# A copy on ScalarE moved behind the scores and exponentials of head 13

## The chip, the cores and the metric

The kernel runs on one core of a Trainium2 chip. A core has engines that each run their own list of instructions in order and meet through semaphores: TensorE (PE in the profile; its weight loads are PEld), VectorE (DVE), ScalarE (ACT), GpSimd (POOL) and SyncE (SP), which here only issues DMAs. Sixteen DMA engines move data between device memory and the core's buffers. The metric is the device time of one execution in microseconds (us); lower is better.

## The reference

Attention with a gate for each of 8 batches and 8 heads (576 positions, head size 64), and then a layer norm and an MLP with a residual on the 512 joined columns:

```python
scores = scale * np.matmul(q, k.transpose(0, 1, 3, 2))
cum = np.cumsum(np.maximum(s, 0.0), axis=-1)
bias = -(cum[:, :, :, None] - cum[:, :, None, :])
scores = np.where(causal, -1e9, scores + np.minimum(bias, 0.0))
attn = softmax(scores)                       # by row
x = join_heads(np.matmul(attn, v))           # (8, 576, 512)
xn = (x - mean) / np.sqrt(var + 1e-6) * g_ln
out = x + np.maximum(xn @ w_ch1, 0.0) @ w_ch2
```

The condensed lines `softmax` and `join_heads` stand for the reference's own lines; inputs and output are float32.

## The kernel before

All of the work is written out by hand as one list of short words, `PLAN` (lines 1274 to 1356). A loop at the end of `fast_path` (1357) takes word after word and calls the function that `STEPS` (1191) has for it. Nothing reorders the instructions later: the order of the words is the order in which each engine gets its instructions, and two steps on different engines are tied only where one reads or overwrites what the other uses. Where an engine's next instruction waits, all of its later ones wait.

Batch 0 is worked in tiles of 128 positions, batch 1 in single heads 8 to 15, batches 2 to 7 in pairs of heads (a burst of scores for two heads at once). Matmuls of the MLP for batches that are done stand between the attention steps, as units in a queue; a word `u` or `U` takes the next one. Eight batches of MLP units follow one another to the end of the kernel.

The words that matter here:

- `d.12`, `d.14`: `scores_d` (420), scores and exponentials of the last 64 positions of two heads: a matmul for each head into the tile `sd`, and one exponential on ACT (line 437).
- `s.12` to `s.15`: `scores` (382), one head's scores: five matmuls (line 390) into three PSUM banks `sa`, `sb`, `sc`, and on ACT one exponential for each (line 401), from the bank into the buffer `er`. There are three banks in all for these tiles, so the scores of one head wait for the exponentials of the head before. For heads 10 and up POOL then puts zeros over the masked part (lines 410 and 440).
- `v.12` and so on: `pv` (573), the product of those exponentials with the values, in `pot` (line 583); `n.12`: its norm on DVE (595 to 604).
- `u`, `U`: one MLP unit. In the first half four matmuls into `ph` (`mlp1`, line 761) and a ReLU on ACT (`u`, line 752) or DVE (`U`, line 750); in the second half four matmuls into `py` (`mlp2`, line 780) and after every fourth unit the output on DVE (`yo`, line 792) and a store.
- `lp.9`: `ld_cast_pair` (185) issues on POOL the loads of the keys and queries of head pair 9 into `kp` and `qp`. Pairs 8 to 11 are the pairs of batch 2. `w2.3` (`ld_w2`, line 255) issues on POOL the load of the last quarter of the second MLP weight.
- `O2.k.9`: `side_two` (342), on the engine named after the colon. It copies a loaded pair so that the two heads lie side by side, into a part of `rowb`; the copy itself is the one line 140, 142 or 144 of `copy_on`. In the profile it is `rowb<-kp` or `rowb<-qp`.
- `F.k.9`: `tr_two` (355), six transposes on PE of that part of `rowb` into `trp` (line 360). `G.k.9`: `evac_two` (365), a copy of `trp` to the place that batch 2's bursts read (`kq<-trp`).
- `lv`, `lr`: loads of value, key and query rows of later batches through SP's queue (line 205). `vm`: `weigh_v` (229) on POOL, value rows times weights into `v_bf` (line 232). `cr`: casts of key or query rows on POOL (line 217).
- `tk.2`: `tail_keys` (502), POOL's copies into `kz` of the last 64 keys of batch 2 (line 144). `sd.2`: `tails` (514), PE's scores from them (line 519); `se.2` and `sm.2`: exponential (532) and mask on POOL. `bm`: POOL's masks of a burst (line 492).
- `B2.8`: `burst` (541), scores of pair 8 (line 548); `bx`: its exponentials (553); `Y.8.0`, `Y.8.1`: the products with the values of its two heads, numbers 16 and 17 (line 627).

In this part of the list `O2.k.9` is the first of eight such copies, one for each of the keys and queries of pairs 8 to 11. It comes right after the copies of head pair 7's transposed queries and ahead of the scores of head 12:

```python
def side_two(kind, g, eng):
    o = (2 * g + "kq".index(kind)) % 4 * 2 * QT * D
    x = rowb.rearrange("p t h c -> p (t h c)")[:, o : o + 2 * QT * D].rearrange(
        "p (t h d) -> p t h d", t=QT, h=2
    )
    copy_on(eng, x[0:QP], ready.pop((kind, g))[0:QP].rearrange("p h (t d) -> p t h d", t=QT))
    sided[kind, g] = x
```

Of the kernel before, what the change touches and what calls it, by code (L numbers as in the profile page):

```python
# [30 lines left out]
def fast_path(  # L31
# [13 lines left out]
    B, H, S, D = q.shape  # L45
# [891 lines left out]
    E = {"A": "act", "D": "dve", "P": "pool"}  # L937
# [241 lines left out]
    def raise_flag(count, ones, n):  # L1179
# [106 lines left out]
        Q.q.5 r.0.2:D B.1.0 s.8 u X.3 S.4.1.0 x.4.1.0 y.3:D Sk xk E.q.5.1:D E.q.5.0:A B.0.0 B.3.0 a3 u  # L1286
        v.8 qu.4 qu.5 Q.k.5 lp.9 E.k.5.0:D u E.k.5.1:D V.4.0 N.4.0 s.9 cr.3.0.1 n.8 V.4.1 N.4.1 Q.q.6
        E.q.6.0:A u B.2.0 d.10 s.10 wr Q.k.6 E.k.6.0:D A.0 v.9 lp.10 w2.2 lr.3.1 E.k.6.1:D n.9 u U
        E.q.6.1:A s.11 Q.k.7 Q.q.7 E.q.7.0:A lp.11 La.6 E.k.7.0:D E.q.7.1:A U U O2.k.9:A E.k.7.1:D v.10
        n.10 cr.3.0.0 U d.12 s.12 U v.11 n.11 ga.1.0.0 A.2 d.14 s.13 u w2.3 B.3.1 v.12 n.12 ga.1.0.3  # L1290
        s.14 O2.k.8:A A.1 me wT lv.2.0 wx vo.2:P U v.13 n.13 ga.1.1.2 s.15 cr.3.1.1 U O2.q.9:A ga.1.0.2
        F.k.8 v.14 vm.2.0:P ga.1.0.1 F.k.9 G.k.9:A n.14 U u A.3 lr.3.2 v.15 cr.3.2.0 O2.k.11:A lv.2.1
        lv.2.2 R vm.2.1:P G.k.8:A ga.1.1.1 u lv.2.3 u O2.q.8:A ga.1.1.3 F.q.9 G.q.9:A n.15 ga.1.2.1
# [260 lines left out]
def kernel(tc, q, k, v, s, g, w1, w2, out):  # L1554
    nc = tc.nc
    with tc.tile_pool(name="flag", bufs=1) as pool:
        flag = pool.tile([1, 1], I32, name="flag")
        bad = fast_path(tc, q, k, v, s, g, w1, w2, out, flag)
        with tc.If(bad > 0, preferred_fallthrough_block=False):
            general_path(tc, q, k, v, s, g, w1, w2, out)  # L1560
# [28 lines left out]
```

## Time and profile before

| what | value |
|---|---|
| median of 3 runs | 351.22 us (349.23, 351.22, 352.59) |
| the profiled execution | 351.01 us, of which the span of the instructions is 349.5 us |
| mean granted TensorE clock in it | 0.987 of full speed |
| read from device memory, written to it | 37.11 MB, 9.44 MB |
| `rowb<-kp` copies on ACT | 4, of 829 to 832 ns |
| exponentials `er<-sa`, `er<-sb`, `er<-sc` | about 0.6 us each, the next starting 0.48 us after |

Busy time of an engine counts its own instructions, not its waits. Times inside the profile are microseconds from the start of the span. The chain of waits is followed back from the last instruction of all: at each step to what released it. A row of a timeline has the start, the duration, the engine, the line, the operation, what it writes and reads with sizes, and in brackets the idle time of the engine before it and what ended that. Matmuls are pipelined, so that the durations of neighbouring rows overlap. The granted clock is the share of full speed that the clock of TensorE had in a stretch; the DMA share is the mean busy share of the 16 DMA engines, which passes 1 where transfers overlap on an engine.

### The profile page before, as it was taken

To read this page: it belongs to the slowest core of one execution; us is meant where nothing else is said; L and a number is where in the kernel's file an instruction comes from. 1 tells how busy PE (TensorE), PEld (TensorE's weight loads), DVE (VectorE), ACT (ScalarE), POOL (GpSimd) and SP (SyncE) were. 2 spreads that over 40 slices of the span, in tenths; PEclk is the share of its full clock that TensorE was granted. 3 is DMA by queue.
4 is the path that set the end of the run, shared out by engine and by line. 5 is a ranking of instruction groups with operands and counts; after the bars stand their busy time and mean duration, and the time that the engine had idled before them with its cause. 6 is when DMAs were issued, how large, how long until landed. Compare 5 with 4: busy or idle time off the path is not lost.

```text
span 349.5 us, 8012 instructions
## 1 busy us (share of the span) xinstructions
PE 334.0 (96%) x3066; PEld 185.7 (53%) x3092; DVE 207.4 (59%) x592; ACT 185.7 (53%) x343; POOL 167.9 (48%) x306
## 2 busy tenths in 40 slices
PE   6999988989999999999999999999999999999994
PEld 2998744545554555545554554555545444444443
DVE  6688894956666577456753765567257714433512
ACT  4688858767773778347665675386534303302200
POOL 8898755877477775865687176440301001000000
PEclk9899998999999999999999999999999999999998
DMA  9999999989997899999766958500230040011022
GB/s 150 182 190 172 202 194 212 188 222 218 221 203 155 210 212 208 194 232 224 164 150 172 216 112 187 123 18 2 89 93 0 3 150 32 14 60 61 0 64 66
DMA packets 147485, 48.61 MB, mean 139 GB/s; under 512 B 135184, under 2 KB 142896, under 8 KB 147440
## 3 DMA queue, kind: packets, MB, share of 16 engines
q1 hardware_dynamic: 121616, 38.34, 50.5%
q0 software_dynamic: 24304, 8.92, 21.5%
q10 hardware_dynamic: 1520, 0.79, 0.9%
q8 instruction: 25, 0.41, 0.5%
q14 instruction: 20, 0.16, 0.2%
HBM read 37.11 MB, written 9.44 MB: 133 GB/s over the span
## 4 chain that ended last, share of the span: by engine, by line
PE 88%; DMA 5%; DVE 2%; issue 1%; ACT 1%; POOL 1%; SPq 0%; ACTq 0%
PE py L780 36%; PE ph L761 32%; PE pot L627 7%; DMA kp<-in_k_dram 4%; PE sa L548 2%; PE ph L1068 2%; PE sc L548 2%; PE sb L548 2%; PE trt L944 1%; DMA c_in<-in_s_dram 1%; PE st L966 1%; PE trp L360 1%; PE pot L583 1%; PE pot L1024 0%; PE st L974 0%
## 5 line engine op out<-in xcount | busy, mean ns | idle before, releaser
L780 PE MATMUL py<-w_bf,hT 128*128 128x512 bf16 (+2 forms) x583 | 128.3, 367 | 2.3 <-DVE yo L792 0.8
L761 PE MATMUL ph<-xT,w_bf 128*128 128x512 bf16 x480 | 110.7, 381 | 0.0
L752 ACT ACTIVATE hT<-ph 128x512 bf16<-128x512 f32 x97 | 58.1, 603 | 81.6 <-PE ph L761 80.2
L780 PEld LDWEIGHTS <-hT 128*128 128x128 bf16 x608 | 56.0, 98 | 61.7 <-issue 1.3
L761 PEld LDWEIGHTS <-w_bf 128*128 128x128 bf16 x544 | 51.2, 98 | 56.8 <-issue 0.6
L492 POOL TENSOR_SCALAR_AFFINE_SELECT er<-er 128x256 bf16<-128x256 bf16 x96 | 38.6, 416 | 60.8 <-ACT er L553 45.8
L792 DVE SCALAR_TENSOR_TENSOR yo<-py,rstd,xb 128x512 f32<-128x512 f32 x32 | 23.9, 750 | 49.8 <-PE py L780 42.1
L750 DVE TENSOR_SCALAR hT<-ph 128x512 bf16<-128x512 f32 x39 | 26.7, 690 | 26.6 <-PE ph L761 25.9
L553 ACT ACTIVATE er<-sb 128x512 bf16<-128x512 f32 x48 | 28.2, 609 | 21.1 <-PE sb L548 20.2
L553 ACT ACTIVATE er<-sa 128x512 bf16<-128x512 f32 x48 | 28.6, 609 | 13.7 <-PE sa L548 10.9
L232 POOL TENSOR_TENSOR v_bf<-rowtmp,wt 128x512 bf16<-128x512 f32 (+1 forms) x30 | 32.0, 1072 | 1.1 <-DMA rowtmp<-in_v_dram 0.9
L553 ACT ACTIVATE er<-sc 128x512 bf16<-128x512 f32 x48 | 28.7, 613 | 4.1 <-PE sc L548 4.1
L627 PEld LDWEIGHTS <-er 128*128 128x128 bf16 x672 | 25.7, 97 | 9.5 <-issue 0.6
L627 PE MATMUL pot<-v_bf,er 128*128 128x66 bf16 x672 | 28.0, 193 | 0.1
L684 POOL TENSOR_TENSOR rstd<-rstd,mhalf 128x4 f32<-128x4 f32 (+1 forms) x8 | 8.8, 1098 | 38.2 <-DVE rstd L683 34.4
L644 DVE TENSOR_REDUCE sums<-pot 128x5 f32<-128x10 f32 x48 | 7.9, 165 | 30.5 <-PE pot L627 30.2
L710 DVE SCALAR_TENSOR_TENSOR xn<-xb,mv,gb 128x512 bf16<-128x512 f32 x28 | 24.0, 858 | 1.0
L669 DVE BATCH_NORM_STATS2 stats<-xb 128x6 f32<-128x128 f32 (+1 forms) x84 | 23.8, 323 | 0.4
L217 POOL CAST kq<-rowtmp 128x512 bf16<-128x512 f32 (+1 forms) x30 | 19.3, 652 | 9.6 <-DMA rowtmp<-in_k_dram 9.4
L647 DVE TENSOR_TENSOR xb<-pot,rinvs 128x256 f32<-128x256 f32 x48 | 20.4, 424 | 1.6
L548 PEld LDWEIGHTS <-kq 64*128 64x128 bf16 x360 | 11.2, 94 | 10.1 <-issue 4.7
L983 ACT ACTIVATE er<-st 128x512 bf16<-128x512 f32 x24 | 13.1, 604 | 3.5 <-PE st L974 2.4
(169 smaller groups left out, 398.3 us busy)
## 6 DMA issues: line engine op xcount, KB each, us to landing
out_dram<-yo SPq DMA_DIRECT2D x32, 256.0 KB
rowtmp<-in_v_dram SPq DMA_DIRECT2D x24, 256.0 KB
rowtmp<-in_k_dram SPq DMA_DIRECT2D x20, 256.0 KB
rowtmp<-in_q_dram SPq DMA_DIRECT2D x20, 256.0 KB
w_bf<-in_moe_w_ch_dram POOLq DMA_DIRECT2D x8, 512.0 KB, 8.6
kp<-in_k_dram POOLq DMA_DIRECT2D x8, 144.0 KB, 10.3
qp<-in_q_dram POOLq DMA_DIRECT2D x8, 144.0 KB, 10.6
v_bf<-in_v_dram POOLq DMA_DIRECT2D x8, 128.0 KB, 7.4
```

What stands on the lines that cost most here:

```text
L232: e.tensor_tensor(out=v_bf[b % 2][0:pn, t, :, 0:D], in0=loaded.pop(("v", b, t))[0:pn], in1=wt[0:pn, t, b, :].unsqueeze(2).to_broadcast([pn ...
L492: nc.gpsimd.affine_select(out=out, in_=out, compare_op=ALU.is_ge, fill=0.0, base=0, pattern=pattern, channel_multiplier=-1,)
L548: nc.tensor.matmul(a, lhsT=lhsT, rhs=rhs, start=True, stop=True)
L553: nc.scalar.activation(out=er[:, 2 * n % 4 + i, o : o + 512], in_=bank["B", n].pop((name, i)), func=ACT.Exp, scale=scale,)
L627: nc.tensor.matmul(pot[:, t, :], lhsT=cols, rhs=v_bf[b % 2][:, kb, h, :], start=(kb == 0), stop=(kb == t),)
L669: nc.vector.bn_stats(out=st[b][:, t, part, :], in_=x_tiles(b)[t][:, lo:hi])
L710: nc.vector.scalar_tensor_tensor(out=xn, in0=tiles[t], scalar=mvs[b][:, t, 0:1] if b > 0 else mean0[:, t : t + 1], in1=gb, op0=ALU.subtrac ...
L750: nc.vector.tensor_scalar_max(out=dst, in0=ph, scalar1=0.0)
L752: nc.scalar.activation(out=dst, in_=ph, func=ACT.Relu)
L761: nc.tensor.matmul(ph, lhsT=w1_bf[:, kd, fb * P : (fb + 1) * P], rhs=xT[:, :, kd, :], start=(kd == 0), stop=(kd == KD - 1),)
L780: nc.tensor.matmul(py[t], lhsT=hT[:, fb, t * P : (t + 1) * P], rhs=w2_bf[:, fb, c0:c1], start=(fb == 0), stop=(fb == FB - 1),)
L792: nc.vector.scalar_tensor_tensor(out=yo, in0=py[t], scalar=rs, in1=x[:, c0:c1], op0=ALU.mult, op1=ALU.add)
```

## The change

One word moves in the list: `O2.k.9:A`, the copy of the keys of head pair 9 (the second pair of batch 2). It goes from its place ahead of `E.k.7.1:D` (DVE's copy of pair 7's keys) to one behind `s.13`. On ACT it passes the exponentials of `d.12`, `s.12`, `d.14` and `s.13`, eight instructions. The words between keep their order, and no function changes. The reader of the copy, `F.k.9`, stays where it is, behind `s.15`.

```diff
-        E.q.6.1:A s.11 Q.k.7 Q.q.7 E.q.7.0:A lp.11 La.6 E.k.7.0:D E.q.7.1:A U U O2.k.9:A E.k.7.1:D v.10
-        n.10 cr.3.0.0 U d.12 s.12 U v.11 n.11 ga.1.0.0 A.2 d.14 s.13 u w2.3 B.3.1 v.12 n.12 ga.1.0.3
+        E.q.6.1:A s.11 Q.k.7 Q.q.7 E.q.7.0:A lp.11 La.6 E.k.7.0:D E.q.7.1:A U U E.k.7.1:D v.10 n.10
+        cr.3.0.0 U d.12 s.12 U v.11 n.11 ga.1.0.0 A.2 d.14 s.13 O2.k.9:A u w2.3 B.3.1 v.12 n.12 ga.1.0.3
         s.14 O2.k.8:A A.1 me wT lv.2.0 wx vo.2:P U v.13 n.13 ga.1.1.2 s.15 cr.3.1.1 U O2.q.9:A ga.1.0.2
         F.k.8 v.14 vm.2.0:P ga.1.0.1 F.k.9 G.k.9:A n.14 U u A.3 lr.3.2 v.15 cr.3.2.0 O2.k.11:A lv.2.1
```

## The prediction

> **What bounds the kernel now.** I began with the shares of busy time and the chain of waits on the page. TensorE (PE) is busy nearly everywhere and carries the chain, but one piece of the chain is no engine's work: the landing of a key pair.
>
> ```profile
> PE 334.0 (96%) x3066; PEld 185.7 (53%) x3092; DVE 207.4 (59%) x592; ACT 185.7 (53%) x343; POOL 167.9 (48%) x306
> ...
> PE 88%; DMA 5%; DVE 2%; issue 1%; ACT 1%; POOL 1%; SPq 0%; ACTq 0%
> PE py L780 36%; PE ph L761 32%; PE pot L627 7%; DMA kp<-in_k_dram 4%; PE sa L548 2%; PE ph L1068 2%; PE sc L548 2%; PE sb L548 2%; PE trt L944 1%; DMA c_in<-in_s_dram 1%; PE st L966 1%; PE trp L360 1%; PE pot L583 1%; PE pot L1024 0%; PE st L974 0%
> ```
>
> So a microsecond taken from a gap of PE shortens the kernel, if no later gap takes its place. Next, ScalarE's (ACT's) timeline around that landing (start, duration, line, what, idle time before and who ended it):
>
> ```profile
> 46.18 1.63 ACT L140 COPY kq<-trqk 64x576 bf16<-64x576 bf16 x2
> 52.03 0.83 ACT L140 COPY rowb<-kp 96x768 bf16<-96x768 bf16 x1 [4.23 <-DMA kp<-in_k_dram]
> 52.89 0.27 ACT L437 ACTIVATE er<-sd 64x128 bf16<-64x128 f32 x1
> 53.06 0.58 ACT L401 ACTIVATE er<-sa 128x512 bf16<-128x512 f32 x1
> ```
>
> The second row is the copy that the change moves. ACT stands 4.23 us before it, and the exponentials of head 12 stand behind it. PE's timeline shows who pays:
>
> ```profile
> 49.49 1.03 PE L761 MATMUL ph<-xT,w_bf 128*128 128x512 bf16 x4
> 50.36 0.62 PE L583 MATMUL pot<-v_bf,er 128*128 128x65 bf16 x15
> 50.81 0.22 PE L426 MATMUL sd<-kq 68*128 68x64 bf16 x2
> 53.69 0.59 PE L390 MATMUL sa<-kq 68*128 68x512 bf16 x1 [2.66 <-ACT er L401]
> ...
> 55.04 1.91 PE L761 MATMUL ph<-xT,w_bf 128*128 128x512 bf16 x4
> 56.75 0.75 PE L583 MATMUL pot<-v_bf,er 128*128 128x65 bf16 x15
> ```
>
> Head 13's scores need a score bank (there are three) that head 12's first exponential frees at 53.64. And what follows is slow: four matmuls of L761 take 1.91 us, before the gap 1.03. The table by stretches (PE busy, granted clock, DMA share, GB/s) gives the reason:
>
> ```profile
> 50.80:53.70 2.90, 0.24 (x9) 0.99 1.24 194
> 53.70:55.20 1.50, 1.50 (x6) 0.50 1.23 196
> 55.20:56.20 1.00, 1.00 (x4) 0.50 1.24 191
> 56.20:57.00 0.80, 0.80 (x7) 0.50 1.26 209
> 57.00:57.50 0.50, 0.50 (x16) 0.97 1.25 235
> ```
>
> The clock is at half from 53.7 to 57.0. The DMA share stays over 1.2 with and without PE: loads flow at their own pace here. The last view is GpSimd's (POOL's) timeline, 12 us on, where one of them is waited for:
>
> ```profile
> 66.11 1.04 POOL L232 TENSOR_TENSOR v_bf<-rowtmp,wt 128x512 bf16<-128x512 f32 x1
> 67.10 1.17 POOL L217 CAST kq<-rowtmp 128x512 bf16<-128x512 f32 x2
> 69.22 2.04 POOL L232 TENSOR_TENSOR v_bf<-rowtmp,wt 128x512 bf16<-128x512 f32 x2 [0.95 <-DMA rowtmp<-in_v_dram]
> 71.28 1.00 POOL L217 CAST kq<-rowtmp 128x512 bf16<-128x512 f32 x1
> 73.07 1.40 POOL L144 COPY kz<-kq 64x256 bf16<-64x256 bf16 x2 [0.80 <-ACT kq L140]
> ```
>
> **The change part by part.** *The wait that goes.* The key pair was issued at 38.47 and landed 13.5 us later, at 51.97. The moved copy comes after eight exponentials. ACT is free at 47.81; PE writes head 12's scores from 48.84 to 49.5, so its exponentials run from about 49.3 (one each 0.48). The tail pair's follows PE's `sd` at 51.03, head 13's three end near 52.9. The copy then starts near 52.7, with its data there for 0.7 us: no wait. PE goes from `sd` (ends 51.03) straight on. From there to the end of head 14's scores (58.16 in the chain) it took 7.13 us. At full clock the same work is scores 0.66, four L761 matmuls 0.86, fifteen L583 matmuls 0.45, scores 0.66, by the chain's pieces at full clock: 2.63. PE gains 4.50 here: 2.66 of waiting and 1.84 of half clock.
>
> The Trainium skill ("TensorE: Matmul & The Clock Gate", Part 1) says that the clock halves after at least one idle window of about 3.4 us, that windows run freely, and that it returns after one busy window. The 3.3 us at half clock agree with the return; the gap of 2.66 is shorter than the page's window and still cost the clock. By its length alone that page would have no penalty and a gain of 2.66 at this place.
>
> *The copy itself.* Its 0.83 us (0.73 to the next start) now stands ahead of a ReLU of the MLP, whose matmuls end near 52.4: it starts at 53.5 instead of 52.5. PE has head 12's second product, head 14's scores and five transposes to do meanwhile (0.45 + 0.66 + 0.45), and the other `ph` bank is free, so I take 0; uncovered it costs 0.7. The copy's reader, the transposes at 62.09, moves to 57.6, 4 us behind the copy's new end at 53.5. Of the next three copies two have their data by 53 and one, issued at 47.21, lands 12.3 us later at 59.5, where ACT wants it at 59.1: 0.4 us, beside waits of 1.53 and 0.75 that ACT has there for PE. Cost 0.
>
> *POOL's queue.* The last quarter of the second MLP weight is issued at 56.64, behind head 13's masks, and moves to 53.4. It landed 8.5 us after its issue, at 65.1, and PE first needs it at 67.54 (the second four of the twelve matmuls from 66.68), which becomes 63.0. If it still lands 8.5 after the issue (61.9), nothing waits; if the queue holds it until 65.1, PE waits 2.1. I take something under 1, nearer the first, because the pair ahead of it on that queue lands at 60.6; either end is absorbed by what follows.
>
> *What is late next.* The rows of batch 2's values come over SyncE's queue. No output stands ahead of them there, and its issues from 38 to 66 take 1.3 to 7.3 us each, since the DMA engines are full. So the third piece still lands at 69.2, wherever PE is. From it POOL runs 2.04 of weighing and 1.00 of casting, to 72.28, and then copies the tail keys (`kz`): before at 73.07, having waited 0.80 for ACT, now at 72.33, done at 73.74. PE's tail scores (L519, before at 77.23) would come at 72.75 and wait 1.0. POOL goes on with the work that lay between 74.54 and 77.23 (2.69), to 76.5, and the masks. Before, it idled 1.14 there for ACT; now ACT is done at 74.7. One tail mask (0.63) and two of head 16's (0.37 each) end at 77.85, head 17's two at 78.6. PE, after the tail scores at 73.8 to 74.0 and 2.7 us of MLP, has the next burst of scores from 76.7 to 77.45 and then waits 0.4 for head 16's masks, and 0.3 for head 17's. Its product with the values of head 17 ends at 79.07, before at 81.82. Of the 4.50 there remain 2.75.
>
> *From there on* the list of who waited for whom has no wait of PE but 0.3 us of issue: nothing gives the rest back and nothing takes more. The profiled execution took 351.01 us (span 349.5 and 1.5 around it), so 348.26; it lies 0.2 under the median 351.22 of the three. I predict 348.3.
>
> **The rivals.** *All of it stays (346.5).* If the value rows land 1.8 us earlier, or more, POOL no longer holds PE, and 351.0 − 4.5 remains. For it: between 64 and 66 the DMA share is only 0.63, so there is room once the weight is through. Against it: SyncE's issues ahead of the piece end when the DMA lets them. Chance 0.20.
>
> *The clock drops again (350.0).* The new gaps (1.0, 0.4, 0.3, perhaps 2.1 at the weight) could cost half clock once more, 1.7 to 1.84. Against it: gaps of 0.47 and 0.84 within 4 us, at 72 and 76, left the clock at 1.00. Chance 0.10.
>
> *Slower (354.5).* The early issue of the weight pushes in front of the value rows. If each of them lands later by the 4.5 us between the pair before the weight (60.6) and the weight (65.1), the third piece lands at 73.7; POOL's chain is 4.5 late against the sum above, 1.75 later than before, and PE's gap of 5.5 at the tail scores costs 1.7 of clock: 351.0 + 1.75 + 1.7 = 354.5. It decides from a landing at 72.0 (69.2 + 2.75) on. For it: between 60 and 62 POOL's queue moved 0.34 MB and SyncE's 0.09, between 62 and 64 SyncE's moved 0.41. Against it: both orders move the same bytes by 64. Chance 0.07. The Trainium skill ("DMA: Bandwidth & Descriptors", "Issuing engines are not separate DMA queues") says that transfers of all issuing engines share the same 16 DMA engines and interleave; by that rule it is this case that threatens the change.
>
> *Nothing comes of it (351).* Head 12's exponentials wait for something else that lands at 52, or the transfer jitters so that the copy still waits. But nothing else of that time is named by the rows. Chance 0.05.
>
> **How the numbers follow.** The forecast has 0.58. Its own bounds are about 1 us either way, for the landing of the value rows: 347.3 to 349.3. The range takes in the full gain and the second loss of clock: 346.3 to 350.6. It leaves out most of the slower case, of no effect, and tails. The runs before spread from 349.2 to 352.6, so 1% is about what a measurement tells from no change; faster by over 1% means under 347.7. That is the full gain (0.20) and a sixth of the forecast (0.10): 0.30. Slower by over 1% means over 354.7: most of the slower case, 0.05. Within: 0.65.
>
> **What would show it.** Right: no idle time of ACT before the `rowb<-kp` copies around 52.7; PE without a gap from 48 to 62 and clock 1.00 from 53.7 to 57.0; the twelve `py` matmuls at 62.2 instead of 66.68; POOL's wait for value rows still ending near 69.2; a new wait of PE at L519 near 73, ended by POOL's `kz`, and one before L627. The last product of head 17 at 79.1. Wrong: PE behind the old times at 82, the clock at 0.50 anywhere between 57 and 90, the copy still waiting for its landing, or a shift of 4.5 at 82.

## The result and the profile after

| | before | changed |
|---|---|---|
| runs beside each other | 16: median 350.28 us (348.59 to 352.59) | 16: median 347.94 us (346.85 to 349.98) |
| ratio, 95% interval | | 0.9931 (0.991 to 0.9952) |
| the profiled execution, its span | 351.01 us, 349.5 us | 346.96 us, 345.5 us |
| mean granted clock in it | 0.987 | 0.993 |

The change made the kernel faster by 0.7% (0.5 to 0.9%); the forecast was 348.3, 0.8% under the median then known. The two profiled executions lie farther apart (4.05 us) than the medians (2.3 us). Both numbers need an explanation. Ratios in this document leave out the few runs that are over 1.5% above the fastest of their kernel, while the medians are of all runs, and a ratio is not the quotient of the medians beside it.

ScalarE's timeline of the changed kernel:

```profile
46.36 1.62 ACT L140 COPY kq<-trqk 64x576 bf16<-64x576 bf16 x2
48.61 0.27 ACT L437 ACTIVATE er<-sd 64x128 bf16<-64x128 f32 x1 [0.63 <-PE sd L426]
48.83 0.60 ACT L401 ACTIVATE er<-sa 128x512 bf16<-128x512 f32 x1
...
52.31 0.83 ACT L140 COPY rowb<-kp 96x768 bf16<-96x768 bf16 x1
53.03 0.61 ACT L752 ACTIVATE hT<-ph 128x512 bf16<-128x512 f32 x1
```

The exponentials of head 12 follow their scores at once, and the copy at 52.31 has no idle time before it. TensorE's rows and its stretches (PE busy, clock, DMA share, GB/s) at the place of the old gap:

```profile
50.38 0.22 PE L426 MATMUL sd<-kq 68*128 68x64 bf16 x2
50.44 0.38 PE L390 MATMUL sa<-kq 68*128 68x512 bf16 x1
...
51.09 1.03 PE L761 MATMUL ph<-xT,w_bf 128*128 128x512 bf16 x4
52.10 0.61 PE L583 MATMUL pot<-v_bf,er 128*128 128x65 bf16 x15
```

```profile
50.80:53.70 2.90, 2.90 (x34) 1.00 1.25 195
53.70:55.20 1.50, 1.50 (x22) 1.00 1.22 193
...
56.20:57.00 0.80, 0.80 (x13) 1.00 1.28 226
```

No gap, and full clock. Four matmuls of L761 take 1.03 us where they took 1.91. From the start of head 12's scores to the start of head 15's it is now 6.67 us (48.41 to 55.08), before 11.03 (48.84 to 59.87): 4.36 us gone. Another 0.43 us of the distance between the two profiled executions arose ahead of head 12's scores (48.41 against 48.84), before the moved copy has any effect.

Not all of it arrives. The chain of waits of the changed kernel leaves TensorE between 44 and 77 (start, duration, what):

```profile
44.28 18.41 DMA rowtmp<-in_k_dram
62.70 5.80 DMA rowtmp<-in_v_dram
68.50 0.07 issue
68.57 2.56 POOL v_bf L232 x2
71.13 0.55 POOL kq L217
71.69 0.35 POOL kz L144
...
75.25 0.60 POOL c L492
75.84 1.46 POOL er L492 x4
77.30 0.04 issue
77.35 0.62 PE pot L627 x15
```

So the loads through SyncE's queue and GpSimd's work on them now set the time, up to head 17's product at 77.35. The rows at that place, first GpSimd's masks and then TensorE's two products with their second parts:

```profile
75.81 1.48 POOL L492 TENSOR_SCALAR_AFFINE_SELECT er<-er 128x256 bf16<-128x256 bf16 x4
```

```profile
76.63 0.60 PE L627 MATMUL pot<-v_bf,er 128*128 128x66 bf16 x14
77.06 0.20 PE L627 MATMUL pot<-v_bf,c 128*128 128x66 bf16 x1
77.35 0.59 PE L627 MATMUL pot<-v_bf,er 128*128 128x66 bf16 x14
```

The same place before:

```profile
81.35 0.19 PE L627 MATMUL pot<-v_bf,c 128*128 128x66 bf16 x1
81.38 0.58 PE L627 MATMUL pot<-v_bf,er 128*128 128x66 bf16 x14
```

The masks end at 77.29, and head 17's product starts 0.29 us after the row ahead of it, before 0.03. TensorE stood only about 0.25 us for them, since it had already lost time at 65. The list of who waited for whom (TensorE, 47 to 90 us) shows that, with a longer first row than before (0.8, one time):

```profile
PE py L780 <- DVE yo L792: 1.2, 2, 0.8
PE trp L360 <- ACT kq L140: 0.5, 1, 0.5
```

### The profile page after: what moved, and what is told of

Same layout as the page of the kernel before. It is cut to its first block, busy times and chain, and to the rows that moved or that the text cites. A ratio compares the mean times of both kernels' runs of the same rounds, so it can differ in the third digit from the quotient of the medians.

```text
span 345.5 us, 8012 instructions
## 1 busy us (share of the span) xinstructions
PE 332.2 (96%) x3066; PEld 185.4 (54%) x3092; DVE 206.4 (60%) x592; ACT 185.3 (54%) x343; POOL 168.0 (49%) x306
## 4 chain that ended last, share of the span: by engine, by line
PE 82%; DMA 8%; SPq 3%; POOL 2%; DVE 2%; issue 1%; ACT 0%
PE ph L761 32%; PE py L780 32%; PE pot L627 7%; DMA rowtmp<-in_k_dram 5%; PE sa L548 2%; SPq L205 2%; DMA rowtmp<-in_v_dram 2%; PE trt L944 1%; DMA c_in<-in_s_dram 1%; PE sc L548 1%; PE sb L548 1%; PE ph L1068 1%; PE st L966 1%; POOL v_bf L232 1%; PE pot L1024 1%
## 5 line engine op out<-in xcount | busy, mean ns | idle before, releaser
L761 PE MATMUL ph<-xT,w_bf 128*128 128x512 bf16 x480 | 109.8, 379 | 0.0
L761 PEld LDWEIGHTS <-w_bf 128*128 128x128 bf16 x544 | 51.0, 98 | 56.3
L627 PEld LDWEIGHTS <-er 128*128 128x128 bf16 x672 | 25.7, 97 | 9.7 <-POOL er L492 0.5
L627 PE MATMUL pot<-v_bf,er 128*128 128x66 bf16 x672 | 28.1, 193 | 0.1
L684 POOL TENSOR_TENSOR rstd<-rstd,mhalf 128x4 f32<-128x4 f32 (+1 forms) x8 | 8.8, 1100 | 38.1 <-DVE rstd L683 35.2
L710 DVE SCALAR_TENSOR_TENSOR xn<-xb,mv,gb 128x512 bf16<-128x512 f32 x28 | 25.0, 891 | 1.0
```

The source lines that it names most:

```text
L627: nc.tensor.matmul(pot[:, t, :], lhsT=cols, rhs=v_bf[b % 2][:, kb, h, :], start=(kb == 0), stop=(kb == t),)
L710: nc.vector.scalar_tensor_tensor(out=xn, in0=tiles[t], scalar=mvs[b][:, t, 0:1] if b > 0 else mean0[:, t : t + 1], in1=gb, op0=ALU.subtrac ...
L761: nc.tensor.matmul(ph, lhsT=w1_bf[:, kd, fb * P : (fb + 1) * P], rhs=xT[:, :, kd, :], start=(kd == 0), stop=(kd == KD - 1),)
```

## The experiments

Three distances measure each profile, all read from the starts of TensorE's rows: **A**, from head 12's scores to head 15's, where the stall lies; **B**, from there to head 16's product (the first L627), where the loads can hold TensorE; **C**, from there to the end of the span. C is 268.5 to 269.2 us in all thirteen profiles: apart from this spread, and from the 0.25 us at head 17's product, which falls into C, nothing is gained or lost later. The time ahead of A is no part of the three; head 12's scores start at 47.65 to 49.41 us, and differ by that between executions of one kernel too (48.84 and 49.26 before, 48.41 and 48.02 changed). The ratios are to the kernel before, run on the same chip in five rounds.

| | A | B | median, us | ratio, 95% interval |
|---|---|---|---|---|
| before | 11.03 | 21.04 | 350.28 | 1 |
| changed | 6.67 | 21.55 | 347.94 | 0.9931 (0.991 to 0.9952) |
| e1 before again | 7.22 | 21.01 | 348.34 | 0.9975 (0.9937 to 1.0013) |
| e2 changed again | 6.67 | 22.58 | 347.71 | 0.9941 (0.9908 to 0.9975) |
| e3 early load | 6.68 | 22.01 | 347.54 | 0.9936 (0.9903 to 0.997) |
| e4 filled gap | 9.38 | 21.02 | 348.97 | 0.9982 (0.9956 to 1.0007) |
| e5 half way | 6.67 | 21.44 | 347.12 | 0.9929 (0.9896 to 0.9961) |
| e6 deviation first | 6.67 | 21.01 | 347.36 | 0.9929 (0.9897 to 0.9962) |
| e7 the same, before | 7.32 | 21.02 | 349.70 | 1.0025 (0.9991 to 1.0059) |
| e8 weight late | 6.67 | 22.45 | 348.03 | 0.9987 (0.9958 to 1.0015) |
| e9 keys later, before | 12.35 | 21.02 | 352.77 | 1.0088 (1.0048 to 1.0128) |
| e10 keys later, changed | 6.84 | 22.46 | 348.26 | 0.9949 (0.9918 to 0.998) |
| e11 e3 and e6 | 6.67 | 22.00 | 347.12 | 0.9914 (0.9886 to 0.9943) |

The kernel before had medians of 350.6 (35 runs beside e1 to e4), 349.62 (35, e5 to e8) and 350.42 (29, e9 to e11).

**e1, the kernel before once more.** No edit.

> The kernel before, unchanged, with a new profile: it shows how much its stall varies. Theory (the copy waits for the landing, head 12's exponentials stand behind it, TensorE stands for a score bank and then runs at half clock): ScalarE's idle time before the first copy of the pair 3.5 to 5 us, TensorE's gap before head 13's scores 2 to 3.5 us, granted clock 0.50 in the 3.4 us behind it; ratio 1.00. Rival (the profiled execution was an exception): a gap under 1 us, or no half clock.

The rival came true for the profile. ScalarE's rows, TensorE's row of head 13 and a stretch of this execution, which took 347.97 us:

```profile
47.21 1.62 ACT L140 COPY kq<-trqk 64x576 bf16<-64x576 bf16 x2
49.80 0.83 ACT L140 COPY rowb<-kp 96x768 bf16<-96x768 bf16 x1 [0.96 <-DMA kp<-in_k_dram]
```

```profile
51.45 0.38 PE L390 MATMUL sa<-kq 68*128 68x512 bf16 x1
```

```profile
53.60:57.00 3.40, 3.40 (x49) 1.00 1.25 198
```

The keys landed at 49.70 and not at 51.94, the wait is 0.96 us, TensorE has no gap that its list of waits shows and keeps its clock; A is still 0.55 us over the changed kernel's. So the stall is not of one size. The runs agree with that: of 115 runs of the kernel before beside these kernels 35 are under 349.2 us and the others reach beyond 352; of 28 of the changed kernel 25 are under it. That the low runs of before are those with a short wait is inferred, from the two profiles of its order with a wait of about 1 us (e1, 347.97 us, and e7, whose span is 346.2 against 349.5) and the one with 4.23 (351.01). The spread of the runs can have other sources too, which no profile here separates.

**e2, the changed kernel once more.** No edit.

> The changed kernel, unchanged, with a new profile. Ratio 0.991 to 0.995. Theory (the value rows' landing caps what is kept): TensorE is 4.5 us ahead at head 14's scores and under 4 us ahead at head 17's product, with a wait for the tail keys or the masks between. Rival (nothing caps it): the lead at 58 us is the lead at 82 us.

GpSimd's rows and TensorE's waits:

```profile
59.70 1.04 POOL L232 TENSOR_TENSOR v_bf<-rowtmp,wt 128x512 bf16<-128x512 f32 x1 [1.05 <-DMA rowtmp<-in_v_dram]
63.56 0.61 POOL L217 CAST kq<-rowtmp 128x512 bf16<-128x512 f32 x1 [2.81 <-DMA rowtmp<-in_k_dram]
64.13 1.04 POOL L684 TENSOR_TENSOR rstd<-rstd,mhalf 128x4 f32<-128x4 f32 x1
```

```profile
62.99 1.89 PE L780 MATMUL py<-w_bf,hT 128*128 128x512 bf16 x8 [0.62 <-DMA w_bf<-in_moe_w_ch_dram]
66.01 1.89 PE L780 MATMUL py<-w_bf,hT 128*128 128x512 bf16 x8 [0.62 <-DVE yo L792]
```

The theory's cap is there: B is 1.54 us longer than in the kernel before. But its place is not the tail keys in this profile. Batch 0's reciprocal deviation (L684) stands on GpSimd behind a cast of key rows that now waits 2.81 us for them; the output `yo` needs the deviation, and TensorE needs the bank that `yo` frees. The other 0.62 is the weight quarter itself.

**e3, the landing made earlier, the copy in its old place.**

```diff
     ld_cast_pair(8)
-    ld_w2(1)
...
-Q.k.5 lp.9 E.k.5.0:D
+Q.k.5 lp.9 w2.1 E.k.5.0:D
```

> The kernel before with the copy in its old place, but the loads of pair 9 issued ahead of the second quarter of the second MLP weight (512 KB, which took 3.4 us of that queue) and not behind it. Theory (the landing is the whole cause): the keys land near 48.5 instead of 52, ScalarE waits under 1 us, no gap of TensorE, no half clock; ratio 0.992 to 0.995, as the change. Rival (the gain comes from the order on ScalarE, or from the last weight quarter's earlier issue, and not from the landing): ratio 0.998 to 1.002.

The keys landed at 46.98; the copy ran at 47.13 with no wait, A is 6.68. The ratio is the change's. With another means against the same wait the same gain comes, in ScalarE's old order: what costs the time is the copy's wait for its landing, and not ScalarE's order by itself.

**e4, the gap filled.** Eleven matmuls into an MLP bank between `d.14` and `s.13`; their result is not used.

```diff
+        w = ptile("m", [P, 512], "fill")
+        for _ in range(11):
+            nc.tensor.matmul(w, lhsT=ident, rhs=w1_bf[:, 0, 0:512], start=True, stop=True)
```

> The kernel before with 11 matmuls of 128x512 that nobody reads put on TensorE between the last tail scores of head pair 7 and head 13's scores, where it stands idle: 2.4 us of work in a gap of 2.66. The wait stays, the clock should not fall. Theory (the half clock costs 1.84 of the 4.50): 348.4 against 350.3, ratio 0.994 to 0.996, clock 1.00 from 53 to 57. Rival (half clock is hidden by waits that come later anyway): ratio 0.999 to 1.002. Rival (the gap is mostly shorter than in the profile): slower, up to 1.005.

```profile
51.26 2.53 PE L860 MATMUL fill<-w_bf,ident 128*128 128x512 bf16 x11
53.63 0.38 PE L390 MATMUL sa<-kq 68*128 68x512 bf16 x1
53.98 0.38 PE L390 MATMUL sb<-kq 68*128 68x64 bf16 x2
54.46 0.38 PE L390 MATMUL sc<-kq 68*128 68x320 bf16 x2
```

```profile
53.60:57.00 3.40, 3.29 (x34) 1.00 1.24 196
```

In TensorE's rows the wait stays (head 13's scores come 4.49 us after head 12's, before 4.85), and the clock stays at 1.00. From head 13's to head 15's scores it takes 4.89 us, before 6.18, changed 4.64. So of the 1.54 us that the change saves here, filling gave back 1.29, and that is what the half clock cost. The other 0.25 stays at full clock: head 13's three groups of scores start 0.35 and 0.48 us apart, in the changed kernel 0.22, because the banks still come free at the pace of head 12's late exponentials. One limit: in this execution the copy waited 3.12 us and not 4.23, so the unfilled gap would have been 2.37 us (51.26 to 53.63) and not 2.66; that 2.37 would have halved the clock is taken over from the profile before. By the time the run decides nothing: 0.9956 to 1.0007 holds the theory's 0.996 and the rival's 1. Where there is no gap the fill should cost its 2.5 us; its lowest run, 348.17 us against 347.62 of the kernel before beside it, fits that but does not show it.

**e5, half the way**, the copy behind `s.12`.

> The kernel before with the copy moved only half the way: behind the scores and exponentials of head 12, ahead of those of head 13. Theory (head 12's exponentials behind the waiting copy are what TensorE lacks): ScalarE is free for the copy near 50.3, the keys land at 49.7 to 51.9, so it waits 0 to 1.6 us; head 13's scores come at once, head 14's at most 1.2 us late; no half clock; start of head 15's scores 6.7 to 7.9 us behind head 12's (before 11.0, changed 6.7); ratio 0.992 to 0.996. Rival (all eight exponentials must be ahead of the copy, the stall only moves): a gap of over 2 us before head 14's scores, half clock behind it, ratio 0.998 to 1.002.

```profile
51.00 0.83 ACT L140 COPY rowb<-kp 96x768 bf16<-96x768 bf16 x1
51.72 0.28 ACT L437 ACTIVATE er<-sd 64x128 bf16<-64x128 f32 x1
```

The keys landed at 50.40, so there was nothing to wait for. A is 6.67: head 12's three exponentials ahead of the copy are enough, when the keys land so.

**e6 and e7, the deviation ahead of the cast**, in the changed kernel and, as a control, in the one before.

```diff
-n.14 U u A.3 lr.3.2 v.15
+n.14 U u A.3 R lr.3.2 v.15
...
-lv.2.2 R vm.2.1:P
+lv.2.2 vm.2.1:P
```

> The changed kernel with batch 0's reciprocal deviation on GpSimd (line 684) ahead of the cast of key rows that it stood behind. In the changed kernel's profiles that cast waits 1.5 to 2.8 us for its rows, and TensorE stands 0.34 and 0.62 + 0.62 us for outputs that need the deviation. Theory (this wait is what the loads take back): no gap of TensorE at 62 to 66, from head 15's scores to the product of head 16 21.0 to 21.2 us (changed: 21.55 and 22.58, before: 21.04); 0.3 to 1.4 us under the changed kernel, ratio 0.989 to 0.993. Rival (the loads' cap sits at the tail keys and the masks, as the prediction had it): 21.5 to 22.6 us as before, ratio as the change, 0.992 to 0.995.

> Control: the same edit on GpSimd in the kernel before, with the copy in its old place. There the cast does not wait for its rows (the stall has given them time). Theory: from head 15's scores to head 16's product 21.0 us as before, ratio 0.998 to 1.002. Rival (the edit is of use by itself): ratio 0.994 to 0.997.

GpSimd's rows of e6:

```profile
61.17 1.05 POOL L684 TENSOR_TENSOR rstd<-rstd,mhalf 128x4 f32<-128x4 f32 x1
63.49 0.61 POOL L217 CAST kq<-rowtmp 128x512 bf16<-128x512 f32 x1 [1.28 <-DMA rowtmp<-in_k_dram]
```

The cast waits as before (1.28 us), but nobody waits for it: B is 21.01, the kernel before's. In the control nothing changes (B 21.02). So the waits for `yo` at 65 and 66 in the changed kernel's two profiles come from the deviation. It does not follow that they are what the loads cost in the end. In this execution TensorE reached head 15's scores 1.00 us later than in the changed kernel's first profile (56.08 against 55.08), while the masks ended at the same time (77.33 against 77.29); in the first profile, without the wait for `yo`, head 17's product would have stood for these masks all the same. Nor does the run test e2's wait for the weight quarter, which did not occur here. The ratio in time, 0.9929, can't be told from the change's 0.9931, as the rival had it. So both the deviation and the tail's masks cap the gain, at nearly the same time: the chain of waits runs over the masks in the first profile of the changed kernel, and over the key rows' cast and the deviation in e2.

**e8, the weight quarter issued later**, the word `w2.3` moved behind `s.14`.

> The changed kernel with the last quarter of the second MLP weight issued behind head 14's masks, near 55.6, and not at 52.8: the wait-free order, but the weight's issue 2.8 us later. Theory (the early weight pushes in front of the rows of SyncE's queue): the key rows' cast on GpSimd starts 1 to 1.5 us earlier (changed 62.9, 63.6), the weight lands at 64 to 65 and TensorE waits up to 2 us for it where the changed kernel had it at 62.2 to 63; ratio 0.993 to 0.998. Rival (the early issue is no matter either way): rows and ratio as the change, 0.992 to 0.995.

```profile
64.15 1.89 PE L780 MATMUL py<-w_bf,hT 128*128 128x512 bf16 x8 [1.28 <-DMA w_bf<-in_moe_w_ch_dram]
```

The weight landed at 64.10, and TensorE waits for it 1.28 us. The key rows' cast started at 62.56, only 0.3 and 1.0 us earlier than in the changed kernel's profiles. That fits the theory in kind. Whether the earlier issue, which the change brings along, is a help on the whole is not shown: B is 22.45, between the changed kernel's 21.55 and 22.58. The interval of the time (0.9958 to 1.0015) lies above the rival's range, holds the theory's upper end and also no gain at all, and overlaps e2's (0.9908 to 0.9975), though not the first result's (0.991 to 0.9952).

**e9 and e10, a larger dose.** The loads of pairs 9 and 10 change places in GpSimd's queue, in the kernel before and in the changed one.

```diff
-Q.k.5 lp.9 E.k.5.0:D
+Q.k.5 lp.10 E.k.5.0:D
...
-A.0 v.9 lp.10 w2.2
+A.0 v.9 lp.9 w2.2
```

> A larger dose: the kernel before, but the loads of pair 9 change places with those of pair 10 in GpSimd's queue, so that the keys that the copy waits for land about 2.1 us later (where pair 10's landed: 54.0). Theory: ScalarE stands 5 to 6.5 us before the copy, TensorE 4 to 5 us, half clock behind it nearly always, and no run in the low cluster (under 349.2): the median 1.5 to 2.5 us over the kernel before, ratio 1.003 to 1.009. Rival (later waits absorb it): ratio 0.998 to 1.002.

> The same later landing in the changed kernel. Theory (behind head 13's exponentials the copy has some 2 us of room): ScalarE waits 0 to 2 us at the copy, head 13's exponentials are done, the next to feel it is head 14's exponentials; TensorE's gap under 1 us, no half clock, ratio against the kernel before 0.993 to 0.998. Rival (the stall has only been moved): a gap of over 2 us and the ratio of the swapped kernel before, 1.003 to 1.009.

e9, ScalarE, TensorE and the stretch behind:

```profile
52.66 0.83 ACT L140 COPY rowb<-kp 96x768 bf16<-96x768 bf16 x1 [4.91 <-DMA kp<-in_k_dram]
```

```profile
54.32 0.59 PE L390 MATMUL sa<-kq 68*128 68x512 bf16 x1 [3.95 <-ACT er L401]
```

```profile
54.30:57.70 3.40, 3.38 (x15) 0.50 1.25 207
```

e10, ScalarE:

```profile
53.11 0.83 ACT L140 COPY rowb<-kp 96x768 bf16<-96x768 bf16 x1 [0.96 <-DMA kp<-in_k_dram]
```

The keys landed at 52.6 in e9 and at 53.0 in e10, earlier than the 54.0 expected, so e9's wait and gap lie just under the expected ranges. In the old order the late keys make the gap 3.95 us, the clock halves, and no run of twelve is under 349.9. In the new order the same keys cost ScalarE 0.96 us at a place where TensorE has its scores already: A grows by 0.17. Nearly the same landing, other place of the copy: 0.9949 and 1.0088, with intervals far apart.

**e11, e3's and e6's edits together**, on the kernel before.

> Both causes taken away by other means: the copy in its old place, pair 9's loads ahead of the second weight quarter, and batch 0's reciprocal deviation ahead of the key rows' cast. Theory: no gap of TensorE from 48 to 66, from head 15's scores to head 16's product 21.0 us; 346.5 to 347.3, ratio 0.988 to 0.993. Rival (the two do not add): as the early load alone, 0.9936.

A is 6.67, but B is 22.00 and not 21.0: the weight quarter landed at 63.9, and TensorE waits 0.79 for it. The ratio 0.9914 is the best of all, yet its interval overlaps those of the change, e3, e5 and e6; that it beats the changed kernel is not shown.

## Why the prediction was right, and where not

*The wait that goes* was right. Removed by the order (the change, e5), by an earlier landing (e3), and made larger (e9), it behaves as the step said. Its size: 4.36 us for 4.50. The sum took 1.97 us at full clock from the start of head 13's scores to head 14's, and the changed kernel took 2.11 (50.44 to 52.55); that is the whole 0.14. The split was off by more: the step put 1.84 to the half clock, and e4 gives 1.29, because the rows at half clock were also waiting for banks (0.25 us in e4). The Trainium skill's figure of a 3.4 us idle window ("TensorE: Matmul & The Clock Gate", Part 1) does not fit as a threshold: a gap of 2.66 us halved the clock, while 1.28 (e8) did not, the granted clock behind it being 1.00. The 3.95 of e9 halved it too, and is longer than that figure.

*The copy itself* at no cost was right: it started at 52.31 (52.7 predicted) and the ReLU behind it made no gap. *The weight* landed at 62.20, nearer to the end of 61.9 that was taken; it held TensorE in e2 by 0.62 us, within the step's "under 1".

*What is late next* was right as a mechanism and wrong in its terms. The chain of waits of the changed kernel runs over the very rows that were named: value rows, GpSimd's weighing, `kz`, masks, head 17's product, which waited about 0.25 us (0.3 predicted). But TensorE did not wait 1.0 at the tail scores: `kz` was ready at 72.49 and not at 73.74. The third piece came at 68.57 and not 69.22, and GpSimd's cast and copies took 0.60 and 0.85 us where 1.00 and 1.40 were taken over from the one profile before; its weighing went the other way, 2.56 for 2.04. And the cap's second place was missed: the deviation on GpSimd behind the key rows' cast. That row (65.02 in the profile before) lay in the timeline that was read, and the step followed only the tail keys. Measured to head 17's product, from head 15's scores, the loads took back 0.76 us in the first profile (22.27 for 21.51) and 1.54 in e2 (23.05), and not 1.75. In all ten profiles that have neither the long stall nor the filled gap, e1 and e7 among them, this product starts at 77.0 to 78.2 us, though head 15's scores start anywhere from 54.3 to 56.5: that fits the step's idea that the loads come at their own time, wherever TensorE is.

*From there on* nothing is lost: C is the same everywhere within 0.6 us, as the step had it.

*How the numbers follow:* 348.3 came from a stall of full size less a cap that was too large. Measured, the stall is of full size in a part of the runs only, and the cap is smaller. The two errors offset each other; that the sum, 348.3 for 347.94, was nearer than its terms is luck. Of the rivals, that all of it stays needs B at 21.0, and no profile of the changed kernel had that, only e6 with its further edit; the clock did not drop again in any profile of the changed order between 48 and 90 us; and the slower case did not come, since GpSimd's work on the third piece started at 68.57 to 69.21 in all of them and never near 72.

What stays open is why the keys land at 49.7 or at 51.9 in the same program. A weight quarter ahead of them on the queue had landed at 41.5 in e1 and at 43.4 in the profile before: the difference arose before 42 us. Its issue on GpSimd already differed by about 1 us (31.66 and 32.63), behind a wait of 0.32 us for an earlier weight load in e1 and of 1.13 in the profile before. It was not followed further.

## What to carry to other kernels

A copy that waits for a transfer holds everything behind it on its engine: put it where the transfer has landed in every profile at hand, and look which engine is fed by what stood behind it, since the price is that engine's gap and half clock, not the copy's wait. When such a wait goes, follow every queue whose pace did not change (here SyncE's loads) to the next reader, on all engines, small instructions such as a deviation included. And before a stall's size is taken from one profile, look at the spread of the runs and take a second profile: a kernel whose runs reach from 347.3 to beyond 352 us may have more than one size of it.

## What was not expected of the hardware

The landing of the same 144 KB load varied by 2.2 us from one execution of the program to another (49.70 and 51.94), of which 0.6 us lay in its issue (37.88 and 38.47). And the price on TensorE grew faster than the wait on ScalarE: a wait of 0.96 us cost 0.55 us of A over the 6.67, one of 4.23 cost 4.36, one of 4.91 cost 5.68.
